# FFN work let in from the 50th piece of attention, and a shorter lag of x's split while attention is alone

## The chip, the cores and the metric

The kernel runs on one core of one Trainium2 chip. The metric is the device time of one execution in microseconds (us), the median of several runs; before the change it is 930.41 us. Five engines work side by side, each taking its own instructions strictly in order: PE (matrix products; its weight loads are listed as PEld), DVE (vector), ACT (scalar, activations), POOL (GpSimd), and SP, which here only issues DMAs. They meet through semaphores.

## What is computed

An attention with a local window of 32 keys on each side and 32 global tokens, over 8 batches and 8 heads, feeds a feed-forward layer (FFN) with an ELU between its two products.

```python
# q_l, k_l, v_l: [8, 8, 512, 64]; q_g, k_g, v_g: [8, 8, 32, 64]
s_g = scale * q_g @ k_all.T                    # global queries see all keys
out_g = softmax(s_g) @ v_all
s_ll = where(abs(i - j) <= 32, scale * q_l @ k_l.T, -1e9)
s_lg = scale * q_l @ k_g.T
out_l = softmax(concat(s_lg, s_ll)) @ concat(v_g, v_l)
x = concat(out_g, out_l)                       # as 4608 tokens of 512
h = x @ w_in                                   # 512 -> 2048
g = where(h > 0, h, exp(min(h, 0)) - 1)
return g @ w_out                               # 2048 -> 512
```

All of it is held to nearly full single precision. The FFN therefore splits each operand into two 16-bit parts (names ending in h and l) and adds three products of them.

## The kernel before

**Attention** is a generator that yields after each small step, here called a piece. A slot is one group of 4 heads with one tile of 128 queries (or with the global queries, a "g" slot); batch 0 and 1 and the first slots of batch 2 are worked one slot at a time, 4 pieces to a slot: scores (`stage_s`, L734, softmax on DVE L746, ACT L752, POOL L758), values (`stage_v`, L795), two transposes (`stage_t` L789 with its copy L791, `stage_u` L721 with its copy L722). The slots overlap: a slot's values come three slots behind its scores. From piece 92 on slots are worked in pairs, 8 pieces to a pair. There are some 328 pieces.

**FFN** is a second generator, `ffn_stream`. It works on 17 blocks of 256 tokens (16 of local tokens, one of the global ones), and for each block on 8 pairs `p` of 128-wide columns of the hidden layer. For a pair come a first product (`ffn1`, 24 matmuls on L316, then ACT L326 to L328, DVE L335, ACT L342, DVE L338) and, two pairs later, a second product (`ffn2`, 12 matmuls on L440); each is 4 steps of the generator. `x` of a block has to be scaled and split into `xh` and `xl` first: `split_x` puts a reduction over partitions (s1), the scale with `xh` on ACT (s2, L562) and `xl` on DVE (s3, L565) into a table of later work, so many ticks ahead, and marks the block as usable at the last of them. A tick is one piece of attention or one step of FFN.

**Weights** arrive as 64-bit floats and are converted by the kernel, in 16 units (8 pairs, `w_in` and `w_out`): a DMA of 1 MB into one of two `raw` buffers (L169), ACT L183, POOL L184, DVE L188 to L195, ACT L199, L208 and DVE L211. Five calls at set pieces (`UNITS`, 0, 1, 8, 18 and 30) start the load of the first and convert the first four units; later calls come each time a credit reaches 14, to which each piece from the 58th on adds 2 and each step of FFN adds 1. The pairs form groups a (pair 0), b (1), c (2, 3), d (4, 5), e (6, 7). A group can be used once its table is made, 17 ticks after its last unit. A block taken up before all tables are there goes through the groups one by one, its partial sums going out to `od` in DRAM and back (L452, L433); there are three such blocks. The others go through in one job (group f), whose second product uses sums of weights (`add_up`, L270 to L283) and is on L475.

**The order of the two** is set by `PACE`, a table of points (piece, FFN steps wanted), and by the loop at the end of `attn_ffn`: `lead[0]` is true while the piece's number is below `PACE[1][0]`, and until then FFN only prepares x; after that, FFN is advanced at each piece until its steps reach the line through the points, or until it has no job. Some helpers ask for `lead[0]`, too: while it is true, values go to PSUM tiles `h` and each second slot's scores to `acc`, which FFN doesn't need yet (else all go to the four tiles `pa`), and the copy of `stage_t` is on DVE (else on ACT, until the last table is there). The written order is then smoothed by the framework's scheduler, which moves instructions between neighbours on each engine, so the order of the built program is looked at as well.

Of the kernel before, what the change touches and what calls it, by code (L numbers as in the profile page):

```python
# [35 lines left out]
AHEAD = 2  # L36


PACE = ((0, 0), (66, 0), (112, 180), (320, 850))
WARM = 10  # L40
CONV = 14
NBL = B * SL // BLK
# [18 lines left out]
def attn_ffn(ctx: ExitStack, tc: tile.TileContext, qT, qgT, kT, vT, w_in, w_out, mask, out):  # L61
# [23 lines left out]
    def defer(n, fn):  # L85
        if n == 0:
            return fn()
        later.setdefault(now[0] + n, []).append(fn)

    def tick():  # L90
        now[0] += 1
        for fn in later.pop(now[0], []):
            fn()
# [5 lines left out]
    lead = [True]  # L99
# [23 lines left out]
    def power(dst, src):  # L123

        dst = dst.bitcast(I32)
        nc.vector.tensor_scalar(dst, src.bitcast(I32), 0x7f800000, None, ALU.bitwise_and)
        nc.vector.tensor_scalar_max(dst, dst, LOW)

    def inverse(dst, src):

        nc.vector.tensor_scalar(dst.bitcast(I32), src.bitcast(I32), TOP, -1.0, ALU.subtract, ALU.mult)

    def all_max(dst, src):

        tp = ps_a.tile([P, 512], F32, name="pa")
        tc.keep_in_program_order(nc.tensor.transpose(tp[:, 0:P], src.to_broadcast([P, P]), ident))
        nc.vector.tensor_reduce(out=dst, in_=tp[:, 0:P], op=ALU.max, axis=AX.X)
# [13 lines left out]
    tab = {}  # L151
# [146 lines left out]
    def ffn_stream():  # L298
# [250 lines left out]
        def split_x(blk):  # L549
            xr, mx, nm = ready[blk]  # L550
            xh = ffn.tile([P, NC, BLK], F16, name="xh", bufs=NX)
            xl = ffn.tile([P, NC, BLK], F16, name="xl", bufs=NX)
            done = []
            xf, hf, lf = (a.rearrange("p c t -> p (c t)") for a in (xr, xh, xl))

            def s1():
                all_max(mx[:, 1:2], mx[:, 0:1])

            def s2():
                power(mx[:, 2:3], mx[:, 1:2])  # L560
                inverse(mx[:, 4:5], mx[:, 2:3])
                nc.scalar.activation(hf, xf, AF.Copy, scale=mx[:, 4:5])  # L562

            def s3():
                nc.vector.scalar_tensor_tensor(out=lf, in0=xf, scalar=mx[:, 4:5], in1=hf,  # L565
                                               op0=ALU.mult, op1=ALU.subtract)

            nc.vector.tensor_reduce(out=mx[:, 0:1], in_=mx[:, 6:6 + nm], op=ALU.max, axis=AX.X)
            for i, fn in ((6, s1), (7, s2), (8, s3), (8 if "f" in tab else 13, lambda: done.append(1))):
                defer(i, fn)  # L570
            return xh, xl, mx, done

# [16 lines left out]
        def load():  # L589
            if "f" in tab:  # L590
                n = state.setdefault("sums", 0)
                first = min((GROUPS["abcde"[step[b]]][0] for b in order if 0 < step[b] < 5), default=NP)
                if n < first and not uses[n] and now[0] >= state.get("next", 0):
                    add_up(n)
                    state["sums"] += 1
                    state["next"] = now[0] + 8
            for blk in order:
                if blk in ready and blk not in xs and not step[blk] and len(xs) < NX:
                    xs[blk] = split_x(blk)
# [367 lines left out]
    f = ffn_stream()  # L967
    units = load_weights()
    done = credit = 0

    def pace(i):
        for (i0, d0), (i1, d1) in zip(PACE, PACE[1:]):
            if i < i1:
                break
        return d0 + (d1 - d0) * (i - i0) / (i1 - i0)

    def convert(n):
        nonlocal credit
        credit += n
        if credit >= CONV:  # L980
            credit -= CONV
            next(units, None)

    def advance():
        nonlocal done
        if next(f):
            tick()
            return False
        done += 1
        convert(1)  # L990
        tick()
        return True

    for i, _ in enumerate(attention()):
        lead[0] = i < PACE[1][0]
        if i in UNITS:
            next(units)
        elif i >= PACE[1][0] - 8:
            convert(2)
        want = pace(i)  # L1000
        if lead[0]:
            next(f)
        if done >= want:
            tick()
        while done < max(want, hold[0]) and advance():
            pass
        if align[0]:
            align[0] = False
            for _ in range(7):
                if "f" not in tab or at[0] == 3 or not advance():  # L1010
                    break
            twice[0] = at[0] == 3
# [60 lines left out]
```

## Time and profile before

| | |
|---|---|
| median of 3 runs | 930.41 us (929.56 to 935.79) |
| profiled execution: span from first to last instruction | 927.3 us |
| PE, DVE, ACT, POOL busy | 878.7, 715.8, 638.8, 172.0 us |
| mean granted TensorE clock | 0.988 |
| DMA | 103.60 MB, 112 GB/s on average |

The profiled execution's own time is not listed beside its span; the span is 3.1 us (0.3%) below the median of the runs. Busy times count each engine's instructions; matmuls overlap, so a busy PE is not PE at its peak. Idle time before an instruction is put down to the event that ended it. In tables by stretch, "(x)" is the number of instructions and PEclk the granted clock as a share of full speed.

### The profile page before, as it was taken

The page shows a single profiled execution, that of the slowest core. Times are in us where ns is not written, and L with a number is a line of the kernel's source. Part 1 is how long each engine was busy: PE and PEld are TensorE (multiplying, and loading weights), DVE is VectorE, ACT ScalarE, POOL GpSimd, SP SyncE. Part 2 cuts the span into 40 slices and gives each one's busy share as a digit, 9 for nine tenths or more (in the row PEclk, how much of TensorE's full clock was granted, in tenths as well). Part 3 has the DMA queues.
Part 4 walks back from the last instruction along what each step waited for, and adds up shares of the span by engine and source line. Part 5 has one row for each costly group of instructions (what it writes and reads, how often), then busy time and mean ns, then how long its engine had stood idle before and what let it go on. Part 6 is the DMA issues. An engine that isn't in the chain of part 4 may idle for free.

```text
span 927.3 us, 26295 instructions
## 1 busy us (share of the span) xinstructions
PE 878.7 (95%) x10809; PEld 725.7 (78%) x10809; DVE 715.8 (77%) x1976; ACT 638.8 (69%) x1457; POOL 172.0 (19%) x221
## 2 busy tenths in 40 slices
PE   6779989899989999999999999999999999999997
PEld 3456656566678888888888888888888888888886
DVE  4988889899976768686787768676878677766566
ACT  4779888675766766666767667676766676656564
POOL 3352344244220101100101001010110011200000
PEclk8999999999999999999999999999999999999999
DMA  7976876523541044012421234104301111000000
GB/s 259 357 264 241 282 245 224 162 92 114 187 148 48 27 148 171 2 70 98 156 71 48 70 126 151 49 25 167 128 29 70 47 47 47 1 24 24 1 24 23
DMA packets 39471, 103.60 MB, mean 112 GB/s; under 512 B 5944, under 2 KB 6584, under 8 KB 39352
## 3 DMA queue, kind: packets, MB, share of 16 engines
q1 hardware_dynamic: 39064, 101.66, 31.3%
q8 instruction: 85, 1.39, 0.6%
q14 instruction: 34, 0.28, 0.1%
q10 hardware_dynamic: 288, 0.26, 0.1%
HBM read 86.70 MB, written 15.20 MB: 110 GB/s over the span
## 4 chain that ended last, share of the span: by engine, by line
PE 40%; DVE 30%; ACT 22%; issue 4%; DMA 3%; POOL 1%; DVEq 0%; SPq 0%; ACTq 0%; POOLq 0%
PE pa L316 17%; PE acc L475 8%; PE h L475 6%; ACT gh L354 5%; ACT p L752 5%; DVE gl L338 4%; DVE gx L335 4%; ACT g L326 2%; ACT g L328 2%; PE pa L795 2%; DVE gx L349 2%; DVE gx L350 2%; PE pa L789 1%; DVE p L746 1%; ACT hs L327 1%
## 5 line engine op out<-in xcount | busy, mean ns | idle before, releaser
L316 PE MATMUL pa<-xh,winh 128*128 128x256 f16 x888 | 242.2, 273 | 0.4 <-DVE xglob L865 0.2
L316 PE MATMUL pa<-xh,winl 128*128 128x256 f16 x888 | 242.0, 273 | 0.0
L316 PE MATMUL pa<-xl,winh 128*128 128x256 f16 x888 | 242.0, 273 | 0.0
L316 PEld LDWEIGHTS <-winh 128*128 128x128 f16 x2160 | 209.1, 98 | 34.2 <-issue 5.2
L354 ACT ACTIVATE gh<-gx,xs 128x896 f16<-128x896 f32 x111 | 115.9, 1044 | 140.5 <-DVE gx L351 140.5
L338 DVE SCALAR_TENSOR_TENSOR gl<-gx,xs,gh 128x896 f16<-128x896 f32 x111 | 132.7, 1196 | 80.2 <-ACT gh L354 80.2
L475 PEld LDWEIGHTS <-gh 128*128 128x128 f16 x1568 | 151.0, 98 | 26.8 <-issue 9.6
L758 POOL TENSOR_TENSOR p<-p,sm 128x512 f32<-128x512 f32 x64 | 73.0, 1144 | 333.5 <-DVE sm L757 303.7
L752 ACT ACTIVATE p<-p,m 128x128 f32<-128x128 f32 x256 | 99.4, 391 | 30.5 <-DVE m L746 30.4
L316 PEld LDWEIGHTS <-winl 128*128 128x128 f16 x1080 | 105.7, 98 | 12.9 <-issue 0.6
L475 PE MATMUL acc<-wouth,gh 128*128 128x256 f16 x336 | 91.8, 273 | 2.3 <-DVE o L448 2.3
L475 PE MATMUL acc<-wouth,gl 128*128 128x256 f16 x336 | 91.6, 273 | 0.1
L475 PE MATMUL acc<-woutl,gh 128*128 128x256 f16 x336 | 91.6, 273 | 0.0
L328 ACT ACTIVATE g<-g 128x512 f32<-128x512 f32 x135 | 85.2, 631 | 0.1
L475 PEld LDWEIGHTS <-gl 128*128 128x128 f16 x784 | 76.7, 98 | 10.2 <-DVE gl L338 1.4
L326 ACT ACTIVATE g<-pa,xs 128x512 f32<-128x512 f32 x111 | 75.8, 682 | 8.9 <-PE pa L316 8.0
L475 PE MATMUL h<-raw,gh 128*128 128x256 f16 x448 | 80.0, 273 | 0.0
L475 PE MATMUL h<-raw,gl 128*128 128x256 f16 x224 | 61.1, 273 | 0.0
L335 DVE SCALAR_TENSOR_TENSOR gx<-g,p 128x512 f32<-128x512 f32 x56 | 38.6, 690 | 28.4 <-ACT g L328 26.9
L335 DVE SCALAR_TENSOR_TENSOR gx<-g,hs 128x512 f32<-128x512 f32 x55 | 39.7, 721 | 26.9 <-ACT g L328 26.1
L795 PEld LDWEIGHTS pa<-pt,v 128*64 128x64 f32 x1728 | 52.9, 138 | 7.3 <-issue 6.3
L795 PE MATMUL pa<-pt,v 128*64 128x32 f32 (+1 forms) x1728 | 56.4, 223 | 0.0
(228 smaller groups left out, 1845.4 us busy)
## 6 DMA issues: line engine op xcount, KB each, us to landing
v<-vT SPq DMA_DIRECT2D x64, 512.0 KB, 4.5
k<-kT SPq DMA_DIRECT2D x32, 640.0 KB, 5.0
q<-qT SPq DMA_DIRECT2D x32, 256.0 KB, 5.8
raw<-w_in SPq DMA_DIRECT2D x8, 1024.0 KB, 5.5
raw<-w_out SPq DMA_DIRECT2D x8, 1024.0 KB, 8.1
out<-o SPq DMA_DIRECT2D x32, 256.0 KB, 2.3
od<-o SPq DMA_DIRECT2D x24, 256.0 KB, 2.6
o<-od SPq DMA_DIRECT2D x24, 256.0 KB, 2.8
```

Of the source, the lines that this page charges most:

```text
L316: nc.tensor.matmul(h[:, j, :], wt[:, c, f], xt[:, c, :], start=k == 0, stop=k == 11)
L326: nc.scalar.activation(g, hf, AF.Relu, scale=sc[:, p:p + 1])
L328: nc.scalar.activation(g, g, AF.Exp, scale=-1.0)
L335: nc.vector.scalar_tensor_tensor(out=out, in0=ins[0], scalar=-1.0, in1=ins[1], op0=ALU.add, op1=ALU.max)
L338: nc.vector.scalar_tensor_tensor(out=dst, in0=src, scalar=sg, in1=hi, op0=ALU.mult, op1=ALU.subtract)
L349: nc.vector.tensor_add(gx[:, 2:4, :], q[:, 0:2], q[:, 2:4])
L350: nc.vector.tensor_sub(gx[:, 5:7, :], q[:, 0:4:2], q[:, 1:4:2])
L354: nc.scalar.activation(gh, gx, AF.Copy, scale=sg)
L475: nc.tensor.matmul(cols, gt, w, start=p == 0 and k == 0, stop=last and k == len(todo) - 1, skip_group_check=True)
L752: nc.scalar.activation(ps[i], ps[i], AF.Exp, bias=m[:, i:i + 1], scale=-1.0, accum_out=s[:, 0, i:i + 1])
L758: nc.gpsimd.tensor_tensor(out=pp, in0=pp, in1=s[:, 1, :].unsqueeze(2).to_broadcast([P, 4, P]), op=ALU.mult)
L795: nc.tensor.matmul(o[:, to:to + n], st["v", g, t][:, 4 * h + w, :], st["pt", g, t][:, h, at:at + n], start=start, stop=True, skip_group_ch ...
```

## The change

`PACE`'s second point moves from piece 66 to piece 50: FFN is let in 16 pieces earlier and its line to piece 112 (180 steps) is flatter. The bound for adding 2 credits a piece was `PACE[1][0] - 8`, which was 58; it becomes the constant `MORE`, which is 58 too. In `split_x` the three steps come 3, 4 and 5 ticks after x instead of 6, 7 and 8, and the block is usable 8 ticks after it instead of 13, as long as `lead[0]` is true.

```diff
-PACE = ((0, 0), (66, 0), (112, 180), (320, 850))
+PACE = ((0, 0), (50, 0), (112, 180), (320, 850))
+MORE = 58
...
-            for i, fn in ((6, s1), (7, s2), (8, s3), (8 if "f" in tab else 13, lambda: done.append(1))):
+            lag, last = (3, 8) if lead[0] else (6, 8 if "f" in tab else 13)
+            for i, fn in ((lag, s1), (lag + 1, s2), (lag + 2, s3), (last, lambda: done.append(1))):
                 defer(i, fn)
...
         lead[0] = i < PACE[1][0]
         if i in UNITS:
             next(units)
-        elif i >= PACE[1][0] - 8:
+        elif i >= MORE:
             convert(2)
```

In the changed kernel, line numbers are one higher from `MORE` on and two higher behind `split_x`.

On PE, the place where the first FFN product stands (`xh`, `winh`), behind the values of a slot of batch 0. Before:

```order
L734 MATMUL pa<-k,q 32x128 x16
L795 MATMUL h<-pt,v 64x32 x2
L734 MATMUL acc<-k,q 32x128 x10
L795 MATMUL h<-pt,v 64x64 x4
L795 MATMUL h<-pt,v 64x32 x4
L795 MATMUL h<-pt,v 64x64 x4
L795 MATMUL h<-pt,v 64x32 x2
L734 MATMUL acc<-k,q 32x128 x6
L316 LDWEIGHTS winh
L316 MATMUL h<-xh,winh 128x256
L789 MATMUL pa<-ident,p_84 128x128 x4
```

Now:

```order
L736 MATMUL pa<-k,q 32x128 x16
L797 MATMUL h<-pt,v 64x32 x2
L797 MATMUL h<-pt,v 64x64 x4
L797 MATMUL h<-pt,v 64x32 x4
L797 MATMUL h<-pt,v 64x64 x4
L797 MATMUL h<-pt,v 64x32 x2
L688 MATMUL pa<-k,qg 32x256
L317 LDWEIGHTS winh
L317 MATMUL h<-xh,winh 128x256
L691 MATMUL pa<-k,qg 32x32
L688 MATMUL pa<-k,qg 32x256
```

The first product now stands among the scores of the global queries of batch 1 (`qg`), earlier in the attention; the 47 that follow it make up two whole pairs, with nothing of attention between them but the rest of those scores, and one reduction.

On ACT, the same place: the second block's `xh`, then what follows (`p` is the softmax, `pt` the copies behind the transposes, `g`, `hs`, `gh` the FFN's). Before:

```order
L562 ACTIVATE xh<-xr,xm 128x1024
L752 ACTIVATE p_85,sm<-p_85,m 128x128 x2
L722 COPY pt<-pa 128x2x4x32
L752 ACTIVATE p_83,sm<-p_83,m 128x128 x2
L828 COPY xr<-h 128x2x128
L752 ACTIVATE p_84,sm<-p_84,m 128x128 x4
L183 ACTIVATE cu<-raw 128x1024
L326 ACTIVATE g<-h,xs 128x512
L327 ACTIVATE hs<-h,xs 128x512
```

Now:

```order
L563 ACTIVATE xh<-xr,xm 128x1024
L327 ACTIVATE g<-h,xs 128x512
L328 ACTIVATE hs<-h,xs 128x512
L329 ACTIVATE g<-g 128x512
L793 COPY pt<-pa 128x2x4x64
L724 COPY pt<-pa 128x2x4x32
L754 ACTIVATE p_85,sm<-p_85,m 128x128
L343 ACTIVATE gh<-g,xs 128x512
```

FFN's activations have moved up between the softmaxes, and with them the larger copy of `stage_t` (L793, L791 before), which stood on DVE here; over the whole program 2 of these copies move from DVE to ACT (56 and 8 instead of 58 and 6).

On SP, the DMAs from the load of the sixth unit's weights on (`raw`; `od` is the partial sums in DRAM, `o` the tile they go out from and come back to; `v`, `k`, `q`, `qg` are attention's operands). Before:

```order
L169 DMA raw<-w_out 128x2x1024
L674 DMA v<-vT 128x1024 x2
L669 DMA qg<-qgT 128x64
L659 DMA k<-kT 128x1280 x2
L169 DMA raw<-w_in 128x4x512
L674 DMA v<-vT 128x1024
L664 DMA q<-qT 128x512 x2
L452 DMA od_1323<-o 128x512
L169 DMA raw<-w_out 128x2x1024
L452 DMA od_1323<-o 128x512
L433 DMA o<-od_1323 128x512 x2
```

Now:

```order
L170 DMA raw<-w_out 128x2x1024
L671 DMA qg<-qgT 128x64
L676 DMA v<-vT 128x1024
L453 DMA od_1149<-o 128x512 x2
L434 DMA o<-od_1149 128x512 x2
L170 DMA raw<-w_in 128x4x512
L453 DMA od_1149<-o 128x512 x2
L676 DMA v<-vT 128x1024
L453 DMA od_1798<-o 128x512
L661 DMA k<-kT 128x1280 x2
L170 DMA raw<-w_out 128x2x1024
```

The next load of weights, and the two loads of `k` that stood ahead of it, now stand behind the first block's partial sums on their way out and back, and `k` behind three more writes of partial sums.

## The prediction

> **What bounds the kernel now.** I read the page's busy shares first, then one table by stretch with its borders at the events that matter (first FFN product, third block's first product, end of the stretch of FFN alone, first product of L475), then the waits of DVE, then single rows. The page's busy shares:
>
> ```profile
> PE 878.7 (95%) x10809; PEld 725.7 (78%) x10809; DVE 715.8 (77%) x1976; ACT 638.8 (69%) x1457; POOL 172.0 (19%) x221
> ```
>
> PE carries the kernel as a whole. By stretch (us of the stretch; then busy us of PE, PEld, DVE, ACT, POOL) it looks otherwise:
>
> ```profile
> 52.00:70.00 18.00, 14.91 (x334) 10.09 (x334) 15.37 (x76) 12.69 (x51) 10.65 (x22) 1.00 0.77 281
> 70.00:83.00 13.00, 12.92 (x156) 10.46 (x157) 12.03 (x33) 11.25 (x33) 4.79 (x5) 1.00 0.78 263
> 83.00:109.00 26.00, 22.20 (x299) 13.57 (x297) 22.56 (x73) 23.33 (x55) 6.77 (x13) 0.93 0.68 248
> 109.00:152.00 43.00, 37.33 (x280) 24.97 (x280) 39.84 (x72) 37.31 (x63) 19.16 (x21) 1.00 0.75 251
> 152.00:180.00 28.00, 23.35 (x222) 14.84 (x221) 25.62 (x57) 21.50 (x42) 8.33 (x12) 0.96 0.61 189
> 180.00:261.00 81.00, 75.78 (x791) 52.52 (x790) 79.50 (x193) 55.05 (x132) 29.38 (x29) 0.99 0.41 141
> 261.00:928.00 667.00, 655.31 (x8160) 576.18 (x8158) 482.84 (x1326) 443.37 (x981) 73.61 (x101) 1.00 0.20 69
> ```
>
> From 261 us on PE is busy 655.3 of the 666 us that remain: it is the bound there. From 52 to 261 us DVE is the busiest engine nearly everywhere (ACT passes it in 83 to 109): 15.37 + 12.03 + 22.56 + 39.84 + 25.62 + 79.50 = 194.9 of 209 us, so it idles 14.1 us: 2.6, 1.0, 3.4, 3.2, 2.4 and 1.5 us by stretch. What the change can win lies in these 14.1 us, and in work that leaves DVE. The border at 261 is the first row of L475, the one at 70 the first row of L316:
>
> ```profile
> 69.66 0.28 PE L316 MATMUL h<-xh,winh 128*128 128x256 f16 x1
> ...
> L475 PE MATMUL acc<-wouth,gh x336: 269/273/283, 260.9 to 920.2; 128*128 128x256 f16 x168
> ```
>
> **What stays.** The built programs hold the same matmuls; three blocks go through the groups one by one in both. How far the early start carries follows from the code: until table c is made FFN can do four first products and two second ones, 24 steps, and then has no job. Credits for the four units of group c are 4 x 14 = 56 = 24 steps + 2 x 16 pieces, so its last unit is called at piece 73 in both kernels, and its table, 17 ticks later with FFN idle, at piece 87. What moves is when the 24 steps are done: at pieces 51 to 59 instead of 67 to 73. At piece 87 the new line wants 107.4 steps and the old one 82.2 (180 x 37/62 and 180 x 21/46), and FFN catches up from 24 without attention: 84 steps instead of 59. At piece 115 both are at 187 steps, and from the last products ahead of the first L475 on, PE's order is the same row for row, DVE's too. So the sum concerns 52 to 261 us alone; the 667 us behind it I put at no change, since PE's own order and 98% share cover them.
>
> **Term 1, copies: -1.3 us.** While `lead[0]` holds, the copy behind the transpose is on DVE; with it ending 16 pieces earlier, 2 of them go to ACT.
>
> ```profile
> L791 DVE COPY pt<-pa x58: 660/684/691, 16.4 to 777.1; 128x512 f32<-128x512 f32 x58
> L791 ACT COPY pt<-pa x6: 569/578/586, 84.8 to 184.4; 128x512 f32<-128x512 f32 x6
> ```
>
> 2 x 0.68 = 1.4 us leave DVE (0.6 each in back-to-back rows, so 1.2 to 1.4) and 2 x 0.58 = 1.2 us come to ACT. They land where ACT has most room: 12.69 of 18 us in 52 to 70. Should ACT be full there in the new order, the gain is nothing.
>
> **Term 2, FFN in the first stretch: -1.3 us.** In 52 to 70 attention is alone and DVE idles 14.6% (2.63 of 18); in 70 to 83, mixed with FFN, 7.5% (0.97 of 13). If 52 to 70 takes over the share of 70 to 83, 18 x 0.071 = 1.3 us go. Bounds: all 2.6 us, or nothing, if new waits come in. The nearest rows for these are DVE's own waits up to 262 us:
>
> ```profile
> DVE mg L696 <- PE pa L689: 8.1, 3, 6.9
> DVE cu L188 <- POOL cu L184: 3.7, 4, 2.2
> DVE xl L565 <- ACT xh L562: 3.1, 3, 2.3
> DVE xglob L835 <- ACT xr L828: 1.9, 4, 1.0
> DVE gl L338 <- ACT gh L342: 1.1, 2, 0.9
> DVE g L335 <- ACT g L328: 0.5, 1, 0.5
> ```
>
> (6.9 of the 8.1 is the start of the kernel.) The waits of a fresh FFN chain, `xl` on `xh`, `gl` on `gh` and `g` on the exponential, are what would take the place: up to 2.3 + 0.9 + 0.5 us once. Attention's next scores, queued behind them on DVE, would wait as long.
>
> **Term 3, what 70 to 83 turns into: +0.7 us.** The FFN that was mixed into it is gone, so it becomes attention with weight units, as 83 to 109 is, where DVE idles 13.2% (3.44 of 26): 13 x (0.132 - 0.075) = 0.7. Bounds 0 and 1.7 (all of 13.2%).
>
> **Term 4, the longer stretch of FFN alone: -0.2 us.** 59 steps took 43 us (109 to 152), 0.73 us each; 25 more are 18 us. They idle 7.3% (3.16 of 43) where the mixture they come out of, 180 to 261, idles 1.9%: 18 x 0.054 = +1.0. Against it, 152 to 180 holds a wait for weights while attention is mixed in, which has a place of its own:
>
> ```profile
> ACT cu L183 <- DMA raw<-w_out: 4.0, 1, 4.0
> ...
> 175.12 1.29 DVE L565 SCALAR_TENSOR_TENSOR xl<-xr,xm,xh 128x1024 f16<-128x1024 f32 x1 [2.28 <-ACT xh L562]
> ```
>
> ACT waited 4.0 us for the load, `xh` stood behind it and DVE waited 2.3 us for that. All units now fall into the stretch of FFN alone, one each 14 steps (14 x 0.73 = 10.2 us) instead of one each 2.4 pieces; half of these 2.4 us gone is -1.2. Bounds: -2.4 + 0 and +1.0 + 4.0 (one more such wait).
>
> **Term 5, POOL beside DVE: +0.4 us.** POOL is busy 10.65 of 18 us (59%) in 52 to 70 and 4.79 of 13 (37%) in 70 to 83. The FFN's DVE instructions now meet the busier POOL, and some rows of theirs are lengthened:
>
> ```profile
> L335 DVE SCALAR_TENSOR_TENSOR g<-g,hs x19: 674/684/1524, 76.9 to 244.7; 128x512 f32<-128x512 f32 x19
> L338 DVE SCALAR_TENSOR_TENSOR gl<-g,xs,gh x24: 726/746/754, 78.8 to 246.6; 128x512 f16<-128x512 f32 x24
> L758 POOL TENSOR_TENSOR p<-p,sm x64: 1038/1040/2072, 14.1 to 769.7; 128x512 f32<-128x512 f32 x64
> ```
>
> The longest L335 takes 0.84 us over the median. I take half of one such case, 0.4 us; bounds 0 and two, 1.7. [...]
>
> **Sum.** -1.3 - 1.3 + 0.7 - 0.2 + 0.4 = -1.7 us: the profiled 927.3 us become 925.6, and the median of the runs, 930.4, becomes 928.7. The moved DMAs I cost at nothing; their cover is the next rival.
>
> **Rival 1: the gaps close altogether.** If ACT's spare 5.3 us in 52 to 70 take up FFN so that ACT no longer tops 83 to 109, 52 to 109 as a whole may idle as little as 180 to 261 does: 7.0 us become 57 x 0.019 = 1.1, -5.9. With -1.3 for the copies and -1.2 for the late weights and none of terms 3 and 5 that is 922.0; with all 2.4 us of those weights, 920.8. For it speaks that ACT and DVE are busy at different times there; against it that the number of pieces in which attention is alone hardly changes (16 + 14 before, 28 now), and its chains (score, exponential, norm, product) leave those gaps.
>
> **Rival 2, slower: SP's queue.** SP issues in order, and the load of the seventh unit's weights now stands behind the first block's partial sums out and back, `k` behind three more writes. In before:
>
> ```profile
> k<-kT SPq DMA_DIRECT2D x32, 640.0 KB, 5.0
> ...
> 58.62 0.63 PE L686 MATMUL pa<-k,qg 64*32 64x256 f32 x4
> ...
> 73.95 0.81 SPq L659 DMA_DIRECT2D k<-kT  x2
> 77.40 0.38 SPq L169 DMA_DIRECT2D raw<-w_in  x1
> ...
> 86.04 0.33 SPq L452 DMA_DIRECT2D od<-o  x1
> ...
> 90.96 2.67 SPq L433 DMA_DIRECT2D o<-od  x2
> ...
> 106.66 0.90 SPq L452 DMA_DIRECT2D od<-o  x2
> ...
> 103.10 0.66 PE L686 MATMUL pa<-k,qg 64*32 64x256 f32 x8
> ```
>
> The read back is issued by 93.6, 24 us after the first product, and the fifth write 37 us after it. With the first product at 58.6 us (PE's order now has it among the scores that began then), the weights are asked for at 82.6 instead of 77.4, and `k`, behind the fifth write, at 95.6 instead of 73.95. It lands in 5.0 us, at 100.6, and is first used at 103.1: 2.5 us of cover are left. If FFN's chain runs later than that, all attention waits for `k`, and ACT, in order, for the weights: up to 5 us each, 928.7 + 10 = 938.7, and past 939.7 where the stretch of FFN alone waits for weights once more (4.0). It decides if the fifth write comes more than 39.5 us behind the first product. Against it: without weight units between, the chain should be shorter than before, not longer.
>
> **Rival 3: the clock.** By the first table PEclk is 0.93 in 83 to 109 and 0.96 in 152 to 180, where 26 x 0.07 = 1.8 and 28 x 0.04 = 1.1 us of full-speed work are lost. If the longer time without FFN brings two more such dips and PE is the bound by then, that is 928.7 + 2.9 = 931.6. Against it: 52 to 70, with attention alone and PE busy 83%, keeps 1.00. [...]
>
> That the change does nothing, since both orders meet again, is the middle of the forecast, 930.4.
>
> **How the numbers follow.** Forecast (DVE's work stays, a few gaps trade places): 0.56, 925 to 932.5. Rival 1: 0.25, 920 to 925, of which 0.11 below 921.1. Rival 2: 0.14, 933 to 943, of which 0.08 above 939.7. Rival 3: 0.05. A measurement of this kernel tells about 1%, 9.3 us, from no change: faster 0.11, same 0.81, slower 0.08. Range 921.5 to 937: it leaves out the lower end of rival 1 (0.11) and the upper half of rival 2 (0.09).
>
> **What would show it.** Term 1: 8 copies L793 on ACT. Term 2: DVE's share from 52 us to the end of the early FFN over 90%. Term 4: no ACT wait over 2 us for weights between the third block's first product and the first of L475. As a whole: the first L476 at 258 to 260 us, and 666 us behind it. Wrong: that row outside 252 to 268 us, a wait of DVE or PE for `k`, or a different length behind it.

## The result, and the profile after

| | before | changed |
|---|---|---|
| median of 11 runs, first session | 931.47 us | 937.37 us |
| ratio to the kernel before, same session [95%] | 1 | 1.0065 [1.0051, 1.008] |
| ratio in two further sessions (E9 and F1 below) | 1 | 1.003 [1.0011, 1.0049]; 1.0038 [1.0015, 1.0061] |
| profiled execution, span | 927.3 us | 933.0 us |
| first product on L317 (L316 before) | 69.66 us | 59.86 us |
| `xl` of the third block | 109.11 us | 115.18 us |
| first product on L476 (L475 before), and what is left behind it | 260.9, 666.4 us | 266.4, 666.6 us |

The change makes the kernel slower by 0.3 to 0.65%, where 0.2% faster was forecast; that is little, but all three intervals lie above 1. The ratios go by the fast runs alone (one execution of the kernel before took 5015.59 us), and are not the quotient of the two medians. The FFN does begin 9.8 us earlier; the third block begins 6.1 us later, and all that follows is 5.5 us late. Behind the first L476 nothing changed. The profile page of the changed kernel has about the same busy times as the one before:

```profile
PE 883.4 (95%) x10809; PEld 730.3 (78%) x10809; DVE 714.2 (77%) x1974; ACT 641.0 (69%) x1459; POOL 168.6 (18%) x221
```

PE's 4.7 us more are for the same 10809 matmuls, at a mean granted clock of 0.981 instead of 0.988. So no work came in, and the place has to be found by stretch. The table by stretch of the changed kernel, with busy us of PE, PEld, DVE, ACT and POOL behind the length:

```profile
52.00:70.00 18.00, 16.68 (x253) 12.60 (x254) 12.84 (x56) 12.63 (x40) 10.42 (x19) 0.91 0.69 252
70.00:83.00 13.00, 12.55 (x141) 8.73 (x139) 8.40 (x22) 12.04 (x27) 3.18 (x5) 1.00 0.36 110
...
83.00:109.00 26.00, 19.19 (x301) 12.98 (x302) 22.42 (x78) 20.77 (x64) 7.41 (x6) 0.87 0.83 283
109.00:180.00 71.00, 61.52 (x539) 41.16 (x538) 64.17 (x128) 57.57 (x96) 33.66 (x43) 1.00 0.72 243
180.00:266.00 86.00, 79.67 (x840) 54.35 (x841) 84.50 (x217) 59.87 (x148) 21.07 (x26) 0.96 0.38 133
```

From 52 to 83 us DVE is busy 21.2 of 31 us, where it was busy 27.4; PE is now busy 29.2. DVE idles 9.8 us there instead of 3.6. In the other stretches its idle time is nearly what it was: 3.6 us (3.4 before) to 109 us, 6.8 (5.5) to 180 us, 1.5 (1.5) to the first L476. Added up, DVE idles 21.7 us from 52 us to the first L476 instead of 14.1, is busy 2.1 us less, and 7.6 - 2.1 is the 5.5 us by which that row is late. Such a sum closes for every engine and doesn't name a cause: by PE's, 3.6 us of the 5.5 are more busy time for the same 2075 matmuls, at a mean clock of 0.96 instead of 0.98, and 1.9 us are idle time. (The busy time is read with some missing records: two more profiles of the changed kernel, E9 and F1 below, show 22.0 and 22.3 us busy from 52 to 83 us, and the first L476 at 263.3 and 264.7.) In the first of these two the clock is whole from 52 to 83 us, and DVE idles 9.0 us there all the same, so the lower clock does not make this gap:

```profile
52.00:83.00 31.00, 28.43 (x401) 20.72 (x403) 22.04 (x77) 25.46 (x68) 13.70 (x23) 1.00 0.59 198
```

What DVE waits for from 52 to 83 us, in us in total, times, and the longest:

```profile
DVE g L336 <- ACT g L329: 2.3, 1, 2.3
DVE sg L709 <- ACT pg L705: 1.4, 1, 1.4
DVE pt L793 <- PE pa L791: 1.3, 1, 1.3
DVE xm L138 <- PE pa L137: 1.3, 1, 1.3
DVE gl L339 <- ACT gh L343: 1.2, 2, 0.6
DVE sm L758 <- ACT p L754: 0.9, 1, 0.9
DVE o L449 <- DMA o<-od: 0.7, 1, 0.7
DVE xl L566 <- ACT xh L563: 0.3, 1, 0.3
```

They add up to 9.4 us, nearly all of the 9.8; the same list of the kernel before adds up to 3.2. No single wait makes up the gap: it is a chain of links, each waiting for the one before, and DVE has no other work to put between. One link, on PE's and then DVE's timeline (start, duration):

```profile
61.60 0.28 PE L317 MATMUL h<-xl,winh 128*128 128x256 f16 x1
...
65.32 0.27 PE L317 MATMUL h<-xh,winl 128*128 128x256 f16 x1
65.43 0.27 PE L137 MATMUL pa<-ident,xm 128*128 128x128 f32 x1
```

```profile
65.74 0.29 DVE L138 TENSOR_REDUCE xm<-pa 128x1 f32<-128x128 f32 x1 [1.31 <-PE pa L137]
66.07 0.15 DVE L127 TENSOR_SCALAR xm<-xm 128x1 int32<-128x1 int32 x1
66.20 0.69 DVE L336 SCALAR_TENSOR_TENSOR g<-g,hs 128x512 f32<-128x512 f32 x1
...
77.06 0.69 DVE L336 SCALAR_TENSOR_TENSOR g<-g,hs 128x512 f32<-128x512 f32 x1 [2.31 <-ACT g L329]
77.67 0.69 DVE L189 TENSOR_SCALAR cu<-cu 128x1024 int32<-128x1024 int32 x1
78.39 1.22 DVE L192 SCALAR_TENSOR_TENSOR cu<-raw,cu 128x1024 int32<-128x1024 int32 x1
```

From 61.6 us on PE does 35 matmuls of L317 in a row, 24 of which give DVE only L336 and L339 (0.69 + 0.75 us) to do. The small product L137 of the reduction stands behind them, and DVE waits 1.31 us for it. The first DVE work on a unit of weights (L189, L192, L196) comes at 77.67 us; in the kernel before, two units lay in this stretch (L188 at 71.38 and at 79.85). FFN's early steps are rich in PE work and poor in DVE work, the units the other way round; in the changed kernel most of the steps run through before the units come.

How the steps are bunched follows from the code. The second block's `x` is taken up at piece 51, when `lead[0]` is already false; so the short lag does not hold for it, and it is usable 13 ticks later, at piece 58. By then the line wants 23 steps and 8 are done, and the other 16 are written in that one piece: their first product is the one at 68.80 us, their last on L441 comes at 81.12 us. The kernel before has its 24 steps four a piece, on pieces 67 to 72.

### The profile page after: what moved, and what is told of

Read it like the earlier page. It is cut to its first block, busy times and chain, and to the rows that moved or that the text cites. A ratio compares the mean times of both kernels' runs of the same rounds, so it can differ in the third digit from the quotient of the medians.

```text
span 933.0 us, 26296 instructions
## 1 busy us (share of the span) xinstructions
PE 883.4 (95%) x10809; PEld 730.3 (78%) x10809; DVE 714.2 (77%) x1974; ACT 641.0 (69%) x1459; POOL 168.6 (18%) x221
## 3 DMA queue, kind: packets, MB, share of 16 engines
q8 instruction: 85, 1.39, 0.6%
## 4 chain that ended last, share of the span: by engine, by line
PE 40%; DVE 29%; ACT 23%; issue 4%; DMA 2%; POOL 1%; DVEq 0%; SPq 0%; ACTq 0%; POOLq 0%
PE pa L317 17%; PE acc L476 8%; PE h L476 6%; ACT p L754 6%; ACT gh L355 5%; DVE gl L339 5%; DVE gx L336 4%; ACT g L327 2%; PE pa L797 2%; ACT g L329 2%; DVE gx L350 2%; PE pa L791 2%; DVE gx L351 2%; DMA raw<-w_in 1%; DVE cu L192 1%
## 5 line engine op out<-in xcount | busy, mean ns | idle before, releaser
L317 PE MATMUL pa<-xh,winh 128*128 128x256 f16 x888 | 242.6, 273 | 0.5 <-DVE xglob L867 0.2
L317 PE MATMUL pa<-xh,winl 128*128 128x256 f16 x888 | 242.3, 273 | 0.0
L317 PE MATMUL pa<-xl,winh 128*128 128x256 f16 x888 | 242.3, 273 | 0.0
L317 PEld LDWEIGHTS <-winh 128*128 128x128 f16 x2160 | 209.4, 98 | 35.4 <-issue 6.8
L339 DVE SCALAR_TENSOR_TENSOR gl<-gx,xs,gh 128x896 f16<-128x896 f32 x111 | 133.0, 1198 | 80.1 <-ACT gh L355 80.1
L476 PEld LDWEIGHTS <-gh 128*128 128x128 f16 x1568 | 151.0, 98 | 24.2 <-issue 7.1
L760 POOL TENSOR_TENSOR p<-p,sm 128x512 f32<-128x512 f32 x64 | 73.0, 1144 | 368.4 <-DVE sm L759 295.6
L317 PEld LDWEIGHTS <-winl 128*128 128x128 f16 x1080 | 105.8, 98 | 13.4 <-issue 0.7
L476 PE MATMUL acc<-wouth,gh 128*128 128x256 f16 x336 | 91.8, 273 | 0.0
L476 PE MATMUL acc<-wouth,gl 128*128 128x256 f16 x336 | 91.6, 273 | 0.1
L476 PE MATMUL acc<-woutl,gh 128*128 128x256 f16 x336 | 91.6, 273 | 0.0
L476 PEld LDWEIGHTS <-gl 128*128 128x128 f16 x784 | 76.7, 98 | 10.2 <-DVE gl L339 1.4
L476 PE MATMUL h<-raw,gh 128*128 128x256 f16 x448 | 80.0, 273 | 0.0
L797 PEld LDWEIGHTS pa<-pt,v 128*64 128x64 f32 x1792 | 56.0, 139 | 15.8 <-ACT pt L724 7.2
L797 PE MATMUL pa<-pt,v 128*64 128x32 f32 (+1 forms) x1792 | 60.3, 224 | 7.0 <-ACT pt L724 6.2
L336 DVE SCALAR_TENSOR_TENSOR gx<-g,p 128x512 f32<-128x512 f32 x56 | 38.6, 690 | 29.6 <-ACT g L329 28.2
L476 PE MATMUL h<-raw,gl 128*128 128x256 f16 x224 | 61.1, 273 | 0.0
L336 DVE SCALAR_TENSOR_TENSOR gx<-g,hs 128x512 f32<-128x512 f32 x55 | 39.7, 721 | 26.9 <-ACT g L329 26.2
```

The lines of the kernel that those rows point to most:

```text
L317: nc.tensor.matmul(h[:, j, :], wt[:, c, f], xt[:, c, :], start=k == 0, stop=k == 11)
L336: nc.vector.scalar_tensor_tensor(out=out, in0=ins[0], scalar=-1.0, in1=ins[1], op0=ALU.add, op1=ALU.max)
L339: nc.vector.scalar_tensor_tensor(out=dst, in0=src, scalar=sg, in1=hi, op0=ALU.mult, op1=ALU.subtract)
L476: nc.tensor.matmul(cols, gt, w, start=p == 0 and k == 0, stop=last and k == len(todo) - 1, skip_group_check=True)
L760: nc.gpsimd.tensor_tensor(out=pp, in0=pp, in1=s[:, 1, :].unsqueeze(2).to_broadcast([P, 4, P]), op=ALU.mult)
L797: nc.tensor.matmul(o[:, to:to + n], st["v", g, t][:, 4 * h + w, :], st["pt", g, t][:, h, at:at + n], start=start, stop=True, skip_group_ch ...
```

## The experiments

Each kernel was run in one of six sessions, with the kernel before beside it on the same chip. Ratios are to that one, with 95% intervals; they can differ from the quotient of the two medians (by 0.0018 in F6, 0.0013 in H1). "Idle" is DVE's idle time in the profiled execution from 52 to 83 us, and from 52 us to the first L475 or L476.

| kernel | median us | ratio [95%] | idle, us | first L475/L476 |
|---|---|---|---|---|
| before | | 1 | 3.6; 14.1 | 260.9 |
| changed | 937.37 | 1.0065 [1.0051, 1.008] | 9.8; 21.7 | 266.4 |
| E2 early steps, units behind them | 937.03 | 1.0059 [1.0035, 1.0084] | 12.3; 24.2 | 267.5 |
| E3 before, units ahead | 933.25 | 1.0021 [0.9996, 1.0045] | 3.6; 15.5 | 262.0 |
| E4 changed, old line from 87 | 933.71 | 1.0028 [1.0005, 1.0051] | 8.0; 19.1 | 263.1 |
| E5 changed, units early | 931.16 | 1.0014 [0.9992, 1.0036] | 4.1; 19.9 | 267.2 |
| E6 = E5 + E4 | 928.74 | 0.9977 [0.996, 0.9993] | 4.1; 18.1 | 260.5 |
| E7 before, new line from 87 | 930.55 | 1.0002 [0.9981, 1.0022] | 4.4; 14.7 | 261.4 |
| E8 changed, old lag | 937.12 | 1.0065 [1.0048, 1.0082] | 10.1; 21.1 | 263.6 |
| E9 changed again | 934.32 | 1.003 [1.0011, 1.0049] | 9.0; 18.5 | 263.3 |
| F1 changed again | 933.84 | 1.0038 [1.0015, 1.0061] | 8.7; 17.8 | 264.7 |
| F4 = E4 again | 933.67 | 1.003 [1.001, 1.0049] | 7.4; 16.3 | 263.4 |
| F5 = E5 again | 932.97 | 1.002 [0.9998, 1.0041] | 5.8; 18.9 | 266.2 |
| F6 = E6 again | 928.31 | 0.9993 [0.9972, 1.0015] | 3.4; 16.6 | 262.5 |
| G1 before, short lag | 929.2 | 1.0003 [0.998, 1.0026] | 3.0; 14.4 | 261.4 |
| G2 before, helpers at 50 | 928.78 | 0.9994 [0.9968, 1.0019] | 7.2; 16.6 | 262.8 |
| G3 early steps over 50 to 66 | 931.07 | 1.0008 [0.9989, 1.0027] | 8.3; 15.7 | 262.1 |
| G4 early steps over 54 to 74 | 928.11 | 0.9982 [0.9962, 1.0001] | 5.2; 16.4 | 259.7 |
| H1 = G4, units behind the steps | 932.32 | 1.0027 [1.001, 1.0043] | 7.3; 20.9 | 264.1 |
| H2 = G4, new line from 87 | 931.03 | 1.0002 [0.9986, 1.0017] | 8.0; 19.7 | 264.4 |

The profiled execution is one of some twelve, so a row's idle time and its median need not be of the same height; ratios decide, and the idle times show where.

**The theory and its rivals.** Cover: FFN's early steps are bound by PE and by the chain through ACT, and need DVE work of other kinds (units of weights, attention) beside them; bunched into pieces 51 to 58, 16 of them in one piece, with one unit among them, they leave DVE idle, and the time is paid for later, where DVE is the bound. Rivals: loads of weights and `k` come late in SP's queue; the stretch of 84 steps of FFN alone costs; the short lag costs; attention costs more since its helpers go over to the four tiles `pa` 16 pieces earlier.

### E2, E3: where the units stand

E2 is the changed kernel, E3 the kernel before, each with the fifth to eighth unit at set pieces: behind the early steps (E2, at ticks 85, 87, 88 and 94 instead of 67, 80, 87 and 94), or ahead of them (E3, at ticks 58, 59, 66 and 91 instead of 64, 72, 82 and 91).

E2:

```diff
-MORE = 58
+MORE = 74
-UNITS = 0, 1, 8, 18, 30
+UNITS = 0, 1, 8, 18, 30, 64, 66, 67, 73
-    done = credit = 0
+    done, credit = 0, -24
```

E3:

```diff
-UNITS = 0, 1, 8, 18, 30
+UNITS = 0, 1, 8, 18, 30, 58, 59, 66, 73
-    done = credit = 0
+    done, credit = 0, -24
-        elif i >= PACE[1][0] - 8:
+        elif i >= 74:
```

> The changed kernel with the four units of group c called at pieces 64, 66, 67 and 73 (changed kernel: 58, 59, 66, 73; before: 64, 68, 70, 73), all later calls as in the changed kernel. Theory A (cover): the time was lost because the weight units no longer lie beside FFN's first 24 steps; from 52 to 83 us PE tops the profile and DVE has too little to do. Then later units make it worse still or leave it: 937 to 942 us. Theory B (loads): the loads of weights come late behind the partial sums on SP; then calls that come later wait less on ACT and lose nothing: 934 to 937. Theory C (the longer stretch of FFN alone from piece 87 on): no change from 937, within 1.

> The kernel before with the units of group c called at pieces 58, 59, 66 and 73, where the changed kernel has them; FFN still from piece 66 on. Theory A: units without FFN beside them cost a part of it, the FFN after them lies alone: 932 to 936 us. Theory B: FFN's partial sums come after the loads, nothing waits: 930 to 932. Theory C: 931, no change.

E2 came out at 1.0059, no better than the changed kernel, and DVE idles 12.3 of the 31 us. Its 937.03 us fit theory C as well as theory A; it moves only one unit out of the steps. E3 lost 0.2%, an interval that reaches 1: units ahead of the steps may cost the kernel before something, at most 0.45%.

### E4, E5, E6, and F1, F4, F5, F6: units or line

E4 brings back the line of before from piece 87 on (59 steps of FFN alone in place of 84). E5 puts units among and ahead of the early steps, at ticks 48, 54 and 60. E6 does both.

E4:

```diff
-PACE = ((0, 0), (50, 0), (112, 180), (320, 850))
+PACE = ((0, 0), (50, 0), (87, 82.2), (112, 180), (320, 850))
```

E5:

```diff
-MORE = 58
+MORE = 74
-UNITS = 0, 1, 8, 18, 30
+UNITS = 0, 1, 8, 18, 30, 48, 52, 54, 73
-    done = credit = 0
+    done, credit = 0, -24
```

> The changed kernel with PACE = ((0, 0), (50, 0), (87, 82.2), (112, 180), (320, 850)): FFN early as changed, but from piece 87 on the wanted steps of the kernel before, so FFN alone runs 59 steps at piece 87 instead of 84. Theory C: the loss was the longer stretch: back to 930 to 933 us. Theories A and B: it was lost before piece 87: 935 to 938.

> The changed kernel with the units of group c called at pieces 48, 52, 54 and 73: as far from FFN's start at 51 as 64, 68, 70 and 73 were from 67, but for the last. Theory A: units lie beside FFN again, most of the 6 us come back: 930 to 933 us, DVE busy over 85% from 52 to 83 us. Theory B: the loads for these units still stand behind partial sums and are now wanted earlier: 936 to 941. Theory C: 937, no change.

> Both repairs at once: units of group c at pieces 48, 52, 54 and 73, and the line of the kernel before from piece 87 on; FFN's first 24 steps early as changed. Theory A+C (the loss is the units that no longer lie beside FFN, some 4.6 us, and the longer stretch of FFN alone, some 2.8 us, each by itself): they add up, 928 to 931 us, at or below the kernel before. If instead each removes the same loss (DVE's idle time moves about, and any repair reaches the same floor): 930 to 933, no better than the units alone.

E4 (933.71 us) fell between what the theories gave it; E5 (931.16 us) and E6 (928.74 us) came out as theory A, or A and C together, had it. The changed kernel itself gave 1.0065 in one session and 1.003 in a later one (E9), so the four were run again, side by side:

> The changed kernel a third time, beside the three others of a square: units of weights late or early (F1, F4 against F5, F6), line of FFN new or old from piece 87 on (F1, F5 against F4, F6). So far it was 1.0065 and 1.003 of the kernel before in two jobs. Cover theory: 1.003 to 1.0065, DVE busy 21 to 22 of the 31 us from 52 to 83 us.

> The changed kernel with the line of before from piece 87 on (82.2 steps wanted at piece 87, 59 steps of FFN alone in place of 84). Cover theory: the line does nothing, the same ratio as F1 within 0.002. Rival (the long stretch of FFN alone costs): 0.003 below F1, as E4 was in the first job.

> The changed kernel with four units of weights moved to pieces 48, 52, 54 and 73, so that two lie beside FFN's 24 steps as they did before. Cover theory: 0.003 to 0.006 below F1, DVE busy about 27 of the 31 us from 52 to 83 us. Rival (the long stretch): the same as F1.

> Both edits. Cover theory: the same as F5 within 0.002. If both effects are real they add: 0.006 or more below F1, and below the kernel before, as E6 was in the second job (0.9977).

In that square the units alone take 0.0018 off the ratio (F1 to F5) and the line alone 0.0008 (F1 to F4), both less than an interval; together 0.0045. That is less for the units than the 0.003 to 0.006 expected, and together between the two expectations. Of these runs E6 and F6 alone have ratios below 1; the intervals of E5 and F5 reach 1. In E6 the stretch from 52 to 83 us is filled again, and a hole comes behind it:

```profile
52.00:83.00 31.00, 26.41 (x346) 19.53 (x346) 26.91 (x82) 23.74 (x64) 13.02 (x23) 0.94 0.64 229
83.00:109.00 26.00, 23.76 (x420) 15.49 (x420) 20.77 (x94) 25.21 (x78) 10.59 (x13) 0.93 0.84 282
```

DVE is busy 26.9 of the 31 us, as expected, but only 20.8 of the next 26 (22.6 before), where the units are missing and ACT is the busiest. Moving units mends a part; it doesn't show by itself that the bunching was the cause.

### E7, E8, E9, G1, G2: what costs nothing

E7 is the kernel before with the changed kernel's line from piece 87 on. E8 is the changed kernel without the short lag, G1 the kernel before with it. E9 is the changed kernel once more. G2 is the kernel before, in which only the helpers are told from piece 50 on that attention is no longer alone.

E7:

```diff
-PACE = ((0, 0), (66, 0), (112, 180), (320, 850))
+PACE = ((0, 0), (66, 0), (87, 107.4), (112, 180), (320, 850))
```

E8, and the other way round G1:

```diff
-            lag, last = (3, 8) if lead[0] else (6, 8 if "f" in tab else 13)
-            for i, fn in ((lag, s1), (lag + 1, s2), (lag + 2, s3), (last, lambda: done.append(1))):
+            for i, fn in ((6, s1), (7, s2), (8, s3), (8 if "f" in tab else 13, lambda: done.append(1))):
```

G2, in the three helpers:

```diff
-            if lead[0] and np_[0] % 8 == 0:
+            if alone[0] and np_[0] % 8 == 0:
...
-            if lead[0]:
+            if alone[0]:
...
+        alone[0] = i < 50
```

> The kernel before, FFN from piece 66 on, but with the changed kernel's line from piece 87 on: FFN alone runs 84 steps there instead of 59. Theory C (the longer stretch costs by itself): 933 to 935 us. If it costs only behind the early start: 930 to 932.

> The changed kernel without the shorter lag of x's split: FFN then begins at piece 55 instead of 51. The lag matters only through when the first 24 steps are done; theory A: they lie nearer to the units, 934 to 937 us. If the short lag itself was what cost (x's split ahead of attention's own work on DVE and ACT): 930 to 933.

> The changed kernel once more, as the measure on this chip for the other three: 935 to 938 us by every theory.

> The kernel before with the shorter lag of x's split alone. Both theories: no change, 0.999 to 1.001, first product of FFN where it was.

> The kernel before, FFN from piece 66 on as there, but the helpers that ask whether attention is alone (the PSUM tiles for values and scores, the engine of the copy) told so only up to piece 50. Cover theory: no loss, 0.999 to 1.001. Rival (attention loses its two further sets of PSUM tiles 16 pieces earlier, and that costs): 1.003 or more, and DVE busy well below 27.4 of the 31 us from 52 to 83 us.

The short lag does not make the loss: G1 has none (1.0003), and E8, without it, is no better than the changed kernel (1.0065, and 0.0035 above E9 of the same session, so the short lag may even help an early start a little). E8's steps are bunched, too, on pieces 55 to 58. E9, at 934.32 us, lies below the 935 to 938 that every theory gave it. The long stretch of FFN alone costs the kernel before nothing (E7 1.0002). The helpers cost nothing in the end (G2 0.9994), against that rival, though not as either theory had it: DVE is busy only 23.8 of the 31 us from 52 to 83 us, and the median doesn't show it. Idle DVE in this stretch alone is thus no measure of the loss, and neither is the sum up to the first L475 or L476: it is 16.6 us here, 16.3 in F4 (1.003) and 18.1 in E6 (0.9977). One profiled execution tells where its time goes; only the ratios tell how much.

One more place asks for `lead[0]`: the parts of a unit of weights that is called while it is true follow one another by one tick, and by two after that. The fifth unit goes over to two ticks in the changed kernel. It does so in G4 below, too, and G4 has no loss.

### G3, G4, H1, H2: the early steps spread out

G3 and G4 let FFN in early, but want its 24 steps over 16 or 20 pieces; the units come by the credit as they fall. G4 does one step a piece, now and then two, with units at 8, 12, 18 and 23 steps. In G3 the second block is usable only at piece 61, so 9 of the steps stand in that piece; in G4 it is taken up while `lead[0]` is still true, and is there in time.

G3:

```diff
-PACE = ((0, 0), (50, 0), (112, 180), (320, 850))
+PACE = ((0, 0), (50, 0), (66, 24), (87, 82.2), (112, 180), (320, 850))
```

G4:

```diff
-PACE = ((0, 0), (50, 0), (112, 180), (320, 850))
+PACE = ((0, 0), (54, 0), (74, 24), (87, 82.2), (112, 180), (320, 850))
```

> The changed kernel with the 24 early steps of FFN wanted over pieces 50 to 66 in place of about 9 pieces, and the line of before from piece 87 on; the units follow the credit, one at 8 and one at 18 steps. Cover theory (PE-heavy steps want the DVE-heavy units and softmax beside them): half of the loss gone, 1.000 to 1.002. Rival (an early start costs however it is spread): 1.003 as with the old line alone.

> FFN from piece 54 on, its 24 early steps spread over 20 pieces, one a piece, with three units among them, line of before from piece 87 on. Cover theory: the loss is gone, 0.996 to 1.001, DVE busy over 26 of the 31 us from 52 to 83 us. Rival (an early start costs however it is spread): 1.002 to 1.004.

Both ratios are as the cover theory had them: 1.0008 over 16 pieces, 0.9982 over 20 (DVE's 25.75 us in G4 are just short of the 26). The kernels to hold them against are E4 and F4, which have the same line from piece 87 on and the steps bunched: 1.0028 and 1.003, with intervals that lie above G4's. FFN in G4 starts as early as in the changed kernel (59.8 us), so an early start as such costs nothing. The first line is G4's stretch from 52 to 83 us, to be held against the first two lines of the changed kernel's table:

```profile
52.00:83.00 31.00, 27.79 (x490) 20.52 (x492) 25.75 (x101) 25.98 (x83) 14.30 (x25) 1.00 0.61 211
83.00:109.00 26.00, 22.94 (x311) 14.46 (x307) 21.62 (x72) 23.07 (x60) 9.06 (x8) 0.93 0.82 295
109.00:180.00 71.00, 64.83 (x511) 43.11 (x508) 65.82 (x137) 58.78 (x105) 34.73 (x39) 0.93 0.72 244
```

DVE is busy 25.75 us instead of 21.2, with 101 instructions instead of 76: attention's work is back beside the steps. H1 then takes the units out from among the steps and leaves the spread; H2 gives G4 the long stretch of FFN alone.

H1, from G4:

```diff
-MORE = 58
+MORE = 82
-UNITS = 0, 1, 8, 18, 30
+UNITS = 0, 1, 8, 18, 30, 72, 74, 75, 81
-    done = credit = 0
+    done, credit = 0, -24
```

H2, from G4:

```diff
-PACE = ((0, 0), (54, 0), (74, 24), (87, 82.2), (112, 180), (320, 850))
+PACE = ((0, 0), (54, 0), (74, 24), (87, 107.4), (112, 180), (320, 850))
```

> G4 (24 early steps of FFN at one a piece, pieces 54 to 74) with its first three units taken out from among these steps and put behind them: the fifth to eighth unit at ticks 76, 78, 79 and 85 in place of 62, 67, 72 and 78. If G4's gain is in the units beside the steps: loss back, 0.003 or more above G4's 0.9982. If it is in the spread, softmax and values being cover enough: within 0.002 of G4.

> G4 with the changed kernel's line from piece 87 on (107.4 steps wanted at piece 87: 84 steps of FFN alone in place of 59). If the long stretch of FFN alone costs something: 0.002 to 0.003 above G4's 0.9982. If not: within 0.0015 of it.

H1 lost G4's gain: 1.0027, its interval above G4's. The place of the units counts, then, and spread alone is not enough. But H1 puts off all later units as well (the ninth is called at piece 88 instead of 80, and the last table comes at step 127 instead of 116), so the share of the first three is not separated from that of the others. The table by stretch of H1 shows where it is paid:

```profile
52.00:83.00 31.00, 28.71 (x490) 20.62 (x486) 23.73 (x108) 25.30 (x81) 15.00 (x25) 0.99 0.59 198
83.00:109.00 26.00, 23.60 (x332) 15.33 (x327) 20.15 (x66) 19.81 (x59) 7.40 (x14) 0.96 0.93 317
109.00:180.00 71.00, 59.69 (x484) 39.45 (x483) 63.85 (x128) 56.38 (x97) 28.61 (x35) 0.94 0.66 216
180.00:264.00 84.00, 76.07 (x791) 52.32 (x790) 83.36 (x197) 60.39 (x139) 30.89 (x26) 1.00 0.44 151
```

DVE is 2.0, 1.5 and 2.0 us less busy than in G4 in the first three stretches, and in the last, where it has 0.6 us of idle time in 84, it is the bound: the first L476 comes at 264.1 instead of 259.7. This although its third block begins earlier (`xl` at 105.5 us against 110.2). What DVE doesn't do early is done where nothing hides it.

H2 against G4, 1.0002 against 0.9982, has overlapping intervals. The long stretch costs nothing in E7, 0.0008 between F1 and F4, 0.0027 between F5 and F6, and H2 lies 0.0020 above G4, the lower end of what was expected if it costs: a share of it in the loss, between nothing and 0.3%, stays open. The same goes for a version better than both: G4 and E6 are faster than the changed kernel, but against the kernel before G4's interval just reaches 1, and E6's gain of 0.2% was 0.07% when it was run again (F6). Shown, then, is that the early steps lose time when they are bunched and lose none when they are spread among units; how the loss is shared between the units, the long stretch and the clock is open.

## Why the prediction was wrong

**What stays: right.** 666.6 us behind the first L476 against 666.4, and 666 to 667 in each of the kernels. The sum did concern 52 us to that row alone. FFN does catch up at piece 87 in both kernels, but because the third block is usable there; table c is made three steps later.

**Term 1: right in kind.** Two copies are now on ACT, and the price is that of the row:

```profile
L793 DVE COPY pt<-pa x56: 670/682/692, 16.1 to 782.8; 128x512 f32<-128x512 f32 x56
L793 ACT COPY pt<-pa x8: 562/575/586, 70.3 to 119.9; 128x512 f32<-128x512 f32 x8
```

But the place was off: the first two copies on ACT stand at 70.31 and 72.96 us, where ACT is busy 12.0 of 13 us, not in 52 to 70 us with its room. And 1.4 us less of work on DVE is a gain only where DVE has no holes, and here it got holes.

**Term 2: the step that failed.** It let 52 to 70 us "take over the share of 70 to 83", 7.5% idle, for -1.3 us. That share was of FFN steps with units of weights among them (units called at 6 and 16 of the 24 steps), and it comes from a row in which PE, with 12.92 of 13 us, is the busiest engine, not DVE; the prediction's first paragraph, which excepts only 83 to 109 us, passed over that. In the changed kernel one is called at step 12 and one behind the last, and DVE's idle time in 52 to 70 us grew from 2.6 to 5.2 us: +2.5 instead of -1.3, and past the upper bound of nothing. The new waits that it named, `xl` on `xh`, `gl` on `gh` and `g` on the exponential, are in the list above with 0.3, 1.2 and 2.3 us (the last of them at 77 us, in the next stretch). They were taken for what might replace the gaps that close; they came on top, with five more beside them.

**Term 3: wrong with it.** It held FFN to be out of 70 to 83 us: the pieces of the early steps (51 to 59) were nearly right, but not the time at which they run. In fact 16 of the 24 early steps stand there, from 68.80 us to 81.5 us on PE (the partial sums' L449 follows at 82.68), and DVE idled 4.6 us there instead of 1.7: +3.6 instead of +0.7. Terms 2 and 3 together were put at -0.6 and are +6.2 us; that is more than the whole loss. (In E9 and F1 they are +5.4 and +5.1 us.)

**Term 4: half.** The 4.0 us wait for weights is gone; from 109 us to the first L476 ACT waits 0.4 us for such loads, below the 2 us named. In its place two shorter ones came earlier, which I hadn't counted:

```profile
89.74 1.15 ACT L184 ACTIVATE cu<-raw 128x1024 f32<-128x1024 f32 x1 [1.57 <-DMA raw<-w_in]
102.32 1.12 ACT L184 ACTIVATE cu<-raw 128x1024 f32<-128x1024 f32 x1 [1.49 <-DMA raw<-w_out]
```

DVE's idle time from 109 to 180 us went from 5.5 to 6.8, 5.5 and 5.2 us in the three profiles, about the -0.2 of the term within what they scatter.

**Term 5: nothing in this profile, but real.** No L336 or L339 was lengthened from 52 to 83 us in the changed kernel. In G4 two of three L339 were (1.39 and 1.61 us against 0.74), and this is told below.

**Rival 1** asked for gaps to close; the opposite came. **Rival 2** had the moment right and the cause not. Its load of weights was computed for 82.6 us and was issued at 82.75:

```profile
81.44 1.21 ACT L200 ACTIVATE raw<-cu 128x1024 f32<-128x1024 f32 x1 [0.70 <-DVE cu L196]
82.55 0.18 ACT L200 ACTIVATION_READ_ACCUMULATOR raw<-cu 128x1 f32 x1
```

```profile
79.96 1.30 SPq L434 DMA_DIRECT2D o<-od  x2
82.75 0.38 SPq L170 DMA_DIRECT2D raw<-w_in  x1
...
89.82 0.87 SPq L661 DMA_DIRECT2D k<-kT  x2
```

The read back ahead of it was issued by 81.3 us. Its buffer came free with ACT's last use of it, at 82.73, and it was issued 0.02 us later: it is the late unit that held the load, not SP's queue. `k` was asked for at 89.8 and not at 95.6, and neither PE nor DVE waited for it. A third `raw` buffer, which would test this directly, was not tried.

**Rival 3**, more dips of the clock, was given 0.05 and 931.6 us. Lower clocks did come with the change (a mean of 0.981 instead of 0.988 in the two profiles), but the gap of 52 to 83 us is there without them (E9: 9.0 us at a clock of 1.00); whether they are a cause of the rest or a companion stays open, as the last section tells.

As to the size: the forecast of 928.7 us is 0.998 of the median that it started from. The three measured ratios have a mean of 1.0044, and so the miss is about 0.6%, some 6 us, the size of the 6.8 us that Terms 2 and 3 are off. The first median, 937.4 us, lies just above the range, the two later ones, 934.3 and 933.8 us, in it.

## What to carry to other kernels

A busy share that is lent from one stretch to another is only good for the same mixture: list what lies beside the moved work in the row that the share is from, and whether it moves along. Work that is heavy on one engine should be spread over the work that is heavy on the other (here one step a piece, with the units among them: 0.9982 in G4, against 1.003 in F4) rather than let in as fast as it is ready; and idle time in one stretch of one profiled execution (7.2 us in G2, without a loss) tells where to look, but is not the price of a change.

## What the runs showed of the hardware that was not expected

**The clock.** Stretches at half the TensorE clock come in the profiles of both kernels (in the kernel before, 0.50 in the windows of 3.41 us from 95.93 and from 177.85 us), and the mean clock differs from run to run (0.936 to 0.992 over the 159 executions below). Windows of the changed kernel with PE's busy us, the granted clock, DMA share and GB/s:

```profile
92.09:95.51 3.42, 1.73 (x34) 1.00 0.83 335
95.51:98.92 3.41, 2.17 (x55) 1.00 0.81 271
98.92:102.33 3.41, 1.86 (x60) 1.00 0.91 323
102.33:105.74 3.41, 1.99 (x30) 0.51 0.57 204
139.88:143.29 3.41, 1.58 (x13) 1.00 0.42 141
143.29:146.70 3.41, 3.41 (x23) 1.00 0.79 239
245.69:249.10 3.41, 0.00 (x0) 1.00 0.32 125
249.10:252.51 3.41, 2.68 (x10) 0.51 0.94 302
```

The window from 245.69 us is wholly idle (PE waited 3.6 us for DVE), and the next is halved (0.51). But the window from 98.92 us, in which PE was busy 1.86 us, is followed by half clock as well (0.51), while that from 139.88 us, busy 1.58, is not (1.00). In this profile, neither idle windows alone nor the busy share of a window tells which it will be. These two differ in what PE did: in the first all matmuls took a part of the array (28 of L797, 128*64, and 32 of L736, 64*32), in the second all took the whole of it (128*128). Whether that decides it is not tested. Over 159 executions of the kernel before, in the five later sessions, the median span is 926.8 us at a mean clock of 0.985 and more (66 runs), 928.9 us from 0.979 to 0.984 (73) and 932.6 us below (20). Over 35 of the changed kernel it is 931.3 us in the middle class (18 runs) and 934.2 in the lowest (16), with one run in the highest: about 2 us more at equal clock, of the 4.4 us between the two mean spans (928.4 and 932.8), and lower clocks more often. So about half of the loss goes with the clock, by these wide classes. Whether waits of PE bring the lower clock, or the lower clock the waits, these runs don't show. A single profile of this kernel can therefore be 2 to 4 us off the median, which is as much as the effects of this study.

**DVE beside POOL.** In G4, L339 (`gl`) took 0.74 us with POOL idle, and 1.39 and 1.61 us when it began beside POOL's L760. DVE's rows, then POOL's:

```profile
70.46 1.39 DVE L339 SCALAR_TENSOR_TENSOR gl<-g,xs,gh 128x512 f16<-128x512 f32 x1
...
76.06 1.61 DVE L339 SCALAR_TENSOR_TENSOR gl<-g,xs,gh 128x512 f16<-128x512 f32 x1
...
81.31 0.74 DVE L339 SCALAR_TENSOR_TENSOR gl<-g,xs,gh 128x512 f16<-128x512 f32 x1
```

```profile
70.26 1.04 POOL L760 TENSOR_TENSOR p<-p,sm 128x512 f32<-128x512 f32 x1 [2.34 <-DVE sm L759]
...
76.08 1.04 POOL L760 TENSOR_TENSOR p<-p,sm 128x512 f32<-128x512 f32 x1 [2.57 <-ACT gh L343]
```

POOL's two end at 71.30 and 77.12; the two L339 end 0.55 us after each, though of the second pair it is DVE's that is recorded first, by 0.02 us. In the kernel before, the two longest L335 up to 200 us (1.52 us, from 133.72 and 152.69 us) began beside POOL's L184 (from 133.07 and 152.27 us) and end 0.54 and 0.53 us after it, but an L338 from 162.67 us took its usual 0.74 us beside another L184, from 162.69 us. Which instructions of POOL go with a longer one on DVE, and why, these rows don't show. Time that DVE spends so counts as busy: against 0.74 us each, G4's 25.75 us hold some 1.5 us of it.
